# Alternating passes over a K/V cache that keep their last blocks, a running softmax by units, and weight products by head group inside the passes

## The chip, the cores and the metric

One core of a Trainium2 chip runs the whole program. The metric is the device time of one execution in microseconds (us). All runs quoted here are of the state "fast"; every ratio is to runs of the kernel before on the same chip, in the same rounds. Differences in us between two changed kernels are differences of medians, often from other rounds and chips; the median of the kernel before moved by less than 3 us between those (2212 to 2215).

Names: PE is TensorE (matmuls and transposes), DVE is VectorE, ACT is ScalarE, POOL is GpSimd. POOL issues the writes of gradients in program order, SP issues the loads. "Granted clock" is the share of full speed that the throttle gave TensorE.

## The reference

One token goes through attention, a squared-ReLU FFN, attention and FFN again, then backward through all of it. Both attention layers use the same weights and the same K/V cache, and so do both FFN layers.

```python
B, Hq, Hkv, Sk, Dh, D, F = 1, 32, 4, 65536, 128, 1024, 3584      # bf16

def attn(x, k_cache, v_cache, wq, wo):          # 8 query heads for each of 4 groups
    q = (x @ wq).reshape(B, 1, Hq, Dh).transpose(0, 2, 1, 3)
    k, v = jnp.repeat(k_cache, 8, axis=1), jnp.repeat(v_cache, 8, axis=1)
    p = softmax(jnp.einsum("bhqd,bhkd->bhqk", q, k) * Dh ** -0.5)
    return jnp.einsum("bhqk,bhkd->bhqd", p, v).transpose(0, 2, 1, 3).reshape(B, 1, Hq * Dh) @ wo

def ffn(x, w1, b1, w2, b2):
    r = relu(x @ w1 + b1)
    return (r * r) @ w2 + b2

def fwd(x, ...):
    x = x + attn(ln(x));  x = x + ffn(ln(x))
    x = x + attn(ln(x));  return x + ffn(ln(x))

out, vjp = jax.vjp(fwd, ...);  return out, *vjp(grad_out)   # gradients of x, K, V, wq, wo, w1, b1, w2, b2
```

K and V have 67 MB each, and so have their gradients. The rest is small, but it sits between the large passes.

## The kernel before

It reads K and V four times. Pass 1 and pass 2 are the forward attention of the two layers; pass 3 is the backward of the second layer (query gradient only). Pass 4 is the backward of the first layer, and it also computes the K and V gradients of both layers and writes them. Between two passes lies a "dense stretch": weight products, layernorms and row products (a weight row times a vector, summed along the row), a chain in which each step needs the one before.

In pass 4 a step handles 8 chunks of 128 cache rows. Gradients are cast from PSUM into a staging tile `gst` and written when it is full; four tiles of 1 MB take turns:

```python
J = 16                                         # chunks of a K/V block: 512 KB, rows of 4 KB in DRAM
stpool = ctx4.enter_context(tc.tile_pool(name=lname + "_st", bufs=4))
def k8(idx):                                   # [cut: query gradient]
    if j0 == 0:
        state["st"] = stpool.tile([P, 2, J, DH], BF, name="gst", tag="gst")
    for half in range(2):
        pgs = [ps_gg(), ps_gg()]               # four PSUM buffers of 512 columns
        # ... two matmuls with 64 partitions, then one cast for each into gst
    if j0 + 8 == J:
        nc.gpsimd.dma_start(out=GKv[g][b], in_=st[:, 0, :, :])
        nc.gpsimd.dma_start(out=GVv[g][b], in_=st[:, 1, :, :])
```

The weight gradients are sums of two outer products (one for each layer). They run in the background of pass 4, one PSUM tile of 512 columns in each step; the two row vectors lie in rows padded with zeros to 128 partitions:

```python
rows = pool.tile([P, 32 * P], BF, name=name, tag=tag)
nc.gpsimd.memset(rows[:, 0:n], 0.0)            # 126 of 128 partitions are zero
...
nc.tensor.matmul(pg[:, 0:nn], lhsT=st["a"][:, kb * P:(kb + 1) * P], rhs=st["b"][:, n0:n0 + nn], ...)
evac(stg[:, n0:n0 + nn], pg[:, 0:nn])
# ... when the row of tiles is complete:
nc.gpsimd.dma_start(out=out_dram[kb * P:(kb + 1) * P, :], in_=stg[:, 0:N])

def bg(i):                                     # called once a step; per_step is 1 here
    if i < 4: return
    for _ in range(per_step):
        t = next(tasks, None)
        if t is not None: t()
```

## Time and profile before

| kernel | us, median (range) | span | bytes moved | granted clock over pass 4 |
|---|---|---|---|---|
| before | 2212 (2208 to 2216) | 2209.8 | 825.6 MB | 0.96 |

The page's row of GB/s (40 equal slices of 55 us) and of TensorE's clock:

```profile
PEclk9999995579999955599999965899999899999976
GB/s 369 359 409 407 406 394 357 372 340 310 407 407 398 387 328 391 295 382 407 406 404 402 396 295 282 282 414 404 353 415 418 373 401 406 413 402 417 412 294 228
```

The plateau of the passes is 404 to 409 GB/s, in pass 4 up to 418; the dips are the dense stretches (282 to 295), the start of pass 2, where nearly all loads are of K (310), and the tail (228). Stretches cut by hand (columns: from and to, length, busy time and instructions of PE, weight loads, DVE, ACT and POOL, then clock, DMA share, GB/s). Here are the third dense stretch and pass 4:

```profile
1277.00:1400.00 123.00, 74.53 (x889) 61.49 (x890) 95.23 (x191) 79.22 (x97) 4.98 (x4) 0.53 0.72 261
1400.00:2128.00 728.00, 603.32 (x8062) 367.50 (x8059) 555.71 (x969) 455.84 (x817) 268.82 (x500) 0.96 1.01 399
```

### The profile page before, as it was taken

What the parts mean: (1) busy time and instruction counts of PE and PEld (TensorE: products, weight loads), DVE (VectorE), ACT (ScalarE), POOL (GpSimd) and SP (SyncE); (2) the same over time, 40 slices, a digit from 0 to 9 for tenths busy, and PEclk for the clock granted to TensorE, in tenths of its full rate; (3) what the DMA queues carried; (4) which work ended last, traced back from release to release, by engine and by line L of the source; (5) the groups of instructions that cost most, each with busy time, mean ns of one, the idle gap of its engine ahead of it and who ended that gap; (6) DMA issues with size and microseconds to landing.
All of it is one profiled execution on the core that took longest, in us unless ns stands there. A gap on an engine that the chain in (4) does not pass through costs nothing. (4 is left out here: it accounts for less than half of the span.)

```text
span 2209.8 us, 69246 instructions
## 1 busy us (share of the span) xinstructions
PE 1712.9 (78%) x30344; PEld 1338.0 (61%) x30344; DVE 1202.4 (54%) x2148; ACT 1002.5 (45%) x1532; POOL 281.4 (13%) x524
## 2 busy tenths in 40 slices
PE   6888876578888863688888866778888878788875
PEld 5877775568777753577777755444454444455542
DVE  3544430445434300753444367877887777777776
ACT  2543440325434400543333357566566566666654
POOL 0000000000000000000000000243333333343320
PEclk9999995579999955599999965899999899999976
DMA  9999999988999999899999977799999999999976
GB/s 369 359 409 407 406 394 357 372 340 310 407 407 398 387 328 391 295 382 407 406 404 402 396 295 282 282 414 404 353 415 418 373 401 406 413 402 417 412 294 228
DMA packets 229106, 825.57 MB, mean 374 GB/s; under 512 B 23748, under 2 KB 23748, under 8 KB 223684
## 3 DMA queue, kind: packets, MB, share of 16 engines
q1 hardware_dynamic: 184836, 655.46, 76.7%
q0 software_dynamic: 43968, 165.70, 18.6%
q8 instruction: 237, 3.88, 0.7%
q14 instruction: 65, 0.53, 0.1%
HBM read 655.37 MB, written 165.69 MB: 372 GB/s over the span
## 5 line engine op out<-in xcount | busy, mean ns | idle before, releaser
L177 DVE COPY kt<-ps_tr 128x1024 bf16<-128x1024 bf16 x482 | 331.6, 688 | 256.5 <-PE ps_tr L459 135.1
L174 ACT CAST gst<-ps_gg 128x512 bf16<-128x512 f32 x607 | 323.5, 593 | 191.7 <-PE ps_gg L789 144.1
L177 DVE CAST gst<-ps_gg 128x512 bf16<-128x512 f32 x417 | 273.0, 686 | 82.1 <-PE ps_gg L789 51.7
L174 ACT COPY kt<-ps_tr 128x1024 bf16<-128x1024 bf16 x158 | 159.9, 1013 | 312.8 <-PE ps_tr L459 149.0
L177 DVE COPY kt<-ps_gr 128x1024 bf16<-128x1024 bf16 x245 | 168.3, 687 | 172.2 <-PE ps_gr L459 97.3
L459 PEld LDWEIGHTS <-kblk 128*128 128x128 bf16 x4096 | 239.8, 99 | 15.6 <-DMA kblk<-in_A_k_cache_dram 13.9
L478 PE MATMUL ps_sc<-L_qpad,kt 128*128 128x64 bf16 x4096 | 202.9, 195 | 59.3 <-DVE kt L177 49.1
L174 ACT COPY kt<-ps_gr 128x1024 bf16<-128x1024 bf16 x139 | 140.7, 1012 | 212.6 <-PE ps_gr L459 106.5
L789 PE MATMUL ps_gg<-GG,xt 64*128 64x512 bf16 x1024 | 193.6, 394 | 43.9 <-ACT og L174 15.1
L723 PEld LDWEIGHTS <-vblk 128*128 128x128 bf16 x2048 | 137.7, 100 | 141.9 <-issue 127.9
L478 PEld LDWEIGHTS <-kt 128*128 128x128 bf16 x4096 | 160.5, 99 | 84.8 <-DVE kt L177 67.7
L522 PEld LDWEIGHTS <-vblk 128*128 128x128 bf16 x4096 | 172.7, 105 | 54.2 <-DMA vblk<-in_A_v_cache_dram 52.0
L723 PE MATMUL ps_tr<-ident_b,vblk 128*128 128x128 bf16 x2048 | 183.1, 226 | 5.7 <-ACT xt L174 4.8
L352 ACT ACTIVATE junka<-mvt_t 128x1024 bf16<-128x1024 bf16 (+2 forms) x88 | 139.9, 1590 | 101.7 <-DVE mvt_t L351 89.4
L756 POOL COPY X<-eT_123 128x200 bf16<-128x200 bf16 x88 | 46.6, 530 | 984.7 <-ACT junka L352 943.2
L459 PE MATMUL ps_tr<-ident_b,kblk 128*128 128x128 bf16 x2048 | 161.1, 223 | 9.9 <-DMA kblk<-in_A_k_cache_dram 7.8
L459 PE MATMUL ps_gr<-ident_b,kblk 128*128 128x128 bf16 x2048 | 159.8, 221 | 0.0
L624 PEld LDWEIGHTS <-vblk 128*128 128x128 bf16 x2048 | 116.8, 99 | 19.5 <-DMA vblk<-in_A_v_cache_dram 14.3
L522 PE MATMUL ps_acc<-eT_124,vblk 128*128 128x64 bf16 x2048 | 103.2, 209 | 27.5 <-DMA vblk<-in_A_v_cache_dram 26.6
L359 PE MATMUL ps_tr<-ident_b,w_slab 128*128 128x128 bf16 x776 | 95.0, 303 | 32.0 <-DMA w_slab<-in_B_w_dram 15.1
L783 PE MATMUL ps_acc<-X,kblk 128*128 128x64 bf16 x2048 | 118.5, 196 | 0.0
L174 ACT CAST og<-ps_gg 128x512 bf16<-128x512 f32 x139 | 81.0, 586 | 80.7 <-DMA out_dram<-og 44.5
(255 smaller groups left out, 2466.7 us busy)
## 6 DMA issues: line engine op xcount, KB each, us to landing
kblk<-in_A_k_cache_dram SPq DMA_DIRECT2D x512, 512.0 KB, 9.1
vblk<-in_A_v_cache_dram SPq DMA_DIRECT2D x512, 512.0 KB, 9.0
out_dram<-gst POOLq DMA_DIRECT2D x256, 512.0 KB, 10.4
w_slab<-in_A_wq_dram SPq DMA_DIRECT2D x32, 1024.0 KB, 5.6
w_slab<-in_A_wo_dram SPq DMA_DIRECT2D x32, 1024.0 KB, 10.1
w_slab<-in_B_w_dram SPq DMA_DIRECT2D x32, 896.0 KB, 7.7
w_slab<-in_B_w_dram SPq DMA_DIRECT2D x21, 1024.0 KB, 8.7
out_dram<-og POOLq DMA_DIRECT2D x60, 256.0 KB, 8.5
```

Of the source, the lines that this page charges most:

```text
L174: nc.scalar.copy(out=out, in_=in_)
L177: nc.vector.tensor_copy(out=out, in_=in_)
L352: nc.scalar.activation(out=self.junka[:, 0:N], in_=t[:, 0:N], func=ACTF.Copy, accum_out=self.y[:, kc:kc + 1])
L359: nc.tensor.transpose(pt[:, i, :], slab[:, (g0 + i) * P:(g0 + i + 1) * P], ident_b[:, :])
L459: nc.tensor.transpose(pt[:, i, :], kb8[:, i, :], ident_b[:, :])
L478: nc.tensor.matmul(ps_s[:, slot:slot + 8, :].rearrange("p a b -> p (a b)"), lhsT=kt[:, i, :], rhs=qpad[:, g, :, :].rearrange("p a b -> p ( ...
L522: nc.tensor.matmul(ps_o[:, :, :].rearrange("p a b -> p (a b)"), lhsT=vb8[:, i, :], rhs=eT[:, g, :, c:c + 8], start=(c == 0), stop=(c == C ...
L624: nc.tensor.transpose(pt[:, i, :], vb8[:, i, :], ident_b[:, :])
L723: nc.tensor.transpose(pt[:, i, :], vb8[:, i, :], ident_b[:, :])
L756: nc.gpsimd.tensor_copy(out=X[:, 0:un1, R2:3 * R], in_=ea)
L783: nc.tensor.matmul(ps_dq[:, :, :].rearrange("p a b -> p (a b)"), lhsT=kb8[:, i, :], rhs=X[:, sl:sl + 2, :].rearrange("p a b -> p (a b)"), ...
L789: nc.tensor.matmul(pgs[t2][:, :], lhsT=xt[64 * t2:64 * t2 + 64, blk0 + half, :], rhs=GG[64 * t2:64 * t2 + 64, :, :, :].rearrange("p a b c ...
```

## The change

The intent: move fewer bytes, in larger pieces, with fewer stretches in which the DMA queue idles. Core of the diff:

```diff
-    J = 16                                    # K/V blocks of 512 KB
+    J = 32                                    # 1 MB, rows of 8 KB
+    SU = min(128, C)                          # softmax unit: V follows K by 23 steps, not 78
+    NKEEP = 6;  NSTREAM = 6                   # 1 MB slots; only the 6 "keep" slots exist in pass 4
+    def plan_keep(p):                         # last blocks of a pass that the next, reversed, reads first
+        if p == 3: return set()
+        last = TOUCH[p][-(NKEEP + 4):]
+        return set([k for k in TOUCH[p + 1] if k in last][:NKEEP])

-        stpool = ...tile_pool(name=lname + "_st", bufs=4)     # 4 x 16 chunks (1 MB)
+        stpool = ...tile_pool(name="b4_st", bufs=2)           # 2 x 32 chunks (2 MB), same bytes
-                pgs = [ps_gg(), ps_gg()]                      # 4 PSUM buffers of 512 columns
+                pg = ps_gg()                                  # 2 of 1024, one cast for both products

-        rows = pool.tile([P, 32 * P], BF, ...)
-        nc.gpsimd.memset(rows[:, 0:n], 0.0)
+        rows = pool.tile([2, 8 * P], BF, ...)                 # two partitions, no padding
+                    og = pool.tile([P, 8 * P], BF, name="og", tag="og", bufs=3)

+    class Background:                         # wq and wo by head group run as "urgent" work inside passes
+        def step(self, i):
+            if i < 2: return
+            while self.urgent:
+                if next(self.urgent[0][1], "end") == "end":
+                    self.urgent.popleft(); continue
+                return                        # urgent work first: no outer product in this step
+            want = self.total * (i - 2) / self.steps
+            while self.normal and self.done < want:           # catch up with the schedule
+                if next(self.normal[0], "end") == "end": self.normal.popleft()
+                else: self.done += 1

+            add_load(pe=nbk * 0.064)          # in the weight products: the chooser of row products sees PE as loaded
```

A row product can be done on DVE, on DVE and ACT, or by transposes on TensorE; the "chooser" picks the form from a running count of each engine's load. A "turn" is the change from one pass to the next, which reads the cache in the reverse order.

## The prediction

> **What bounds the kernel.** Bytes. The page gives 825.6 MB in a span of 2209.8 us, 374 GB/s. Busy table by stretches:
>
> | stretch | us | GB/s | DMA share |
> |---|---|---|---|
> | pass 1 and start | 370 | 388 | 0.99 |
> | dense 1-2 | 93 | 355 | 0.94 |
> | pass 2 | 362 | 371 | 0.97 |
> | dense 2-3 | 121 | 339 | 0.91 |
> | pass 3 | 331 | 400 | 1.02 |
> | dense 3-4 | 123 | 261 | 0.72 |
> | pass 4 | 728 | 399 | 1.01 |
> | tail | 82 | 228 | 0.63 |
>
> Inside passes the plateau is 405-407 GB/s with PE 83-86% busy: the DMA engines bind. A step of 24 transposes and matmuls takes PE 0.91 us at best (timeline at 950 us), its data 1.29 us. All bytes at 407 GB/s would take 2028 us; some 180 us are lost in dense stretches, V-only ends (323-331 GB/s), K-only beginnings (281-356) and the tail.
>
> **What the change does.**
> 1. Six kept 1 MB blocks at each of three turns: 18.9 MB fewer reads, 46 us at 407 GB/s; total 807 MB.
> 2. Softmax per 128 chunks: V lags K by 23 steps, not 78, so K-only and V-only stretches nearly vanish (about 35 us of lost DMA time). Price: statistics 16 times a pass, not 4. The present ones make PE wait under 2 us each. ACT is under half busy there: off the critical path.
> 3. Three of four head groups of wq and wo, and the output's w2 product, go into the passes. No byte disappears, but each dense stretch shrinks from 31-39 MB to 18.8 MB (46 us of DMA) beside a chain of layernorms, broadcasts and row products, which I estimate from the timeline's pieces (w1 product 6.4 us, 28 row products 22, layernorm 4-5) at 45, 52 and 78 us. A third is loaded at its start; six further blocks can follow, except before pass 4, whose six slots hold kept blocks. Idle DMA: 5, 8 and 40 us.
> 4. The tail keeps one group of four: 82 -> 30 us.
> 5. Rows of 8 KB instead of 4 KB for K, V and their gradients. The Trainium skill ("DMA: Bandwidth & Descriptors", "Why small descriptors are slow") states a fixed cost per packet. The trace agrees: a 1 MB wo slab of 2 KB rows lands every 2.71 us (387 GB/s), a 0.92 MB w1 slab of 7 KB rows every 2.17 us (422). I count +1.5% (estimate) in passes; wq and its gradient fall to 2 KB rows, -5% on 42 MB.
> 6. Pass 4 evacuates 1024 columns at once (512 casts, not 1024): off the critical path.
>
> **Sum** (estimate; K/V at 412 GB/s, 2 KB rows at 380-390): pass 1 370, pass 2 343, pass 3 362, dense 194, pass 4 745 (304 MB), tail 30: about 2040 us, 8% less. Range 1965 to 2120. Faster by over 2%: 0.94; within 2%: 0.04; slower by over 2%: 0.02.
>
> **What would show it.** Bytes near 807 MB; plateau 410 to 425 GB/s in passes; dense stretches of 45 to 80 us, the third worst with DMA share under 0.6; no 50 us stretch of V-only matmuls; tail near 30 us.
>
> **What would make it wrong.** PE is in order: sixteen statistics chains and in-pass weight products could stall it beyond the 0.38 us of slack per step, leaving passes at 380 GB/s. Two 2 MB gradient buffers in pass 4 could make evacuation wait for writes. Kept blocks may idle the queue at a pass's start, giving their gain back. If 8 KB rows reach 423 GB/s everywhere, about 1990.

## More of the kernel before

Pass 4 has the DMA engines busy from end to end. The waits for buffers on their way out are small there (table of waits: engine, line, what it waited for, us in total, times, longest):

```profile
PE ps_gg L837 <- ACT gst L174: 48.9, 126, 3.6
ACT gst L174 <- DMA out_dram<-gst: 40.1, 21, 4.0
ACT og L174 <- DMA out_dram<-og: 33.2, 22, 2.8
DVE gst L177 <- DMA out_dram<-gst: 23.0, 16, 3.8
DVE og L177 <- DMA out_dram<-og: 21.2, 12, 2.5
```

No single wait of these is longer than 4.0 us.

## The result, and the profile after

The changed kernel took 2180 us (median of 4; 2177.5 to 2181.5) beside 2212. The ratio is 0.985, with a 95% interval of 0.984 to 0.987. That is 1.5% faster where 8% was predicted. 806.5 MB were moved, as predicted.

| stretch | before, us | predicted | after, us |
|---|---|---|---|
| passes 1 to 3, with the start | 1063 | 1075 | 1066 |
| three dense stretches | 337 | 194 | 246 (76, 76, 94) |
| pass 4 | 728 | 745 | 838 |
| tail | 82 | 30 | 28 |

Nearly all of the miss is in pass 4 (93 us over the prediction) and in the dense stretches (52 us over). The page:

```profile
PEclk9999998599999966999999667888888878887888
GB/s 383 418 416 416 418 416 402 310 345 415 419 415 417 417 377 264 406 414 418 416 416 419 315 112 359 318 346 369 386 356 357 347 364 364 379 354 349 396 353 249
```

Passes 1 to 3 confirm the large rows: their plateau is 414 to 419 GB/s where it was 404 to 409, some 2.5% more. From slice 25 on, in pass 4, there is no plateau at all: 318 to 396 GB/s, with TensorE's clock at 0.7 to 0.8 in the row of tenths. Pass 4 by the stretch view:

```profile
1312.00:2150.00 838.00, 688.08 (x8015) 421.26 (x8015) 562.51 (x793) 521.86 (x566) 204.59 (x364) 0.84 0.92 358
```

The DMA share fell from 1.01 to 0.92: the queue has less to do than it could. DVE and ACT are busy for 1084 us together against 1012, only 7% more, in a stretch 15% longer. But their waits for staging have grown (the first two lines: 154 us, where it was 63), and the single waits of TensorE for their casts are longer:

```profile
ACT gst L143 <- DMA out_dram<-gst: 89.9, 26, 6.7
DVE gst L146 <- DMA out_dram<-gst: 64.4, 18, 7.0
PE ps_gg L829 <- ACT gst L143: 56.6, 38, 5.5
PE ps_gg L870 <- ACT gst L143: 22.4, 17, 6.0
PE ps_gg L870 <- DVE gst L146: 16.0, 10, 6.3
```

A cast waits for a gradient write and TensorE waits for the PSUM buffer of that cast. In such a wait the trace shows nothing else on TensorE (7.01 us in the timeline under f1_cap), so the transposes and products that would free K/V blocks wait too. The chain of waits that ended last, which the page could follow back for some 27% of the span, has the writes of K/V gradients as its largest part. (In the kernel before the chain breaks off after 3% of the span, so it is no measure there.)

```profile
DMA out_dram<-gst 10%; PE ps_gg L829 2%; PE ps_tr L769 2%; ACT gst L143 2%; PE ps_gg L870 1%; PE ps_sc L787 1%; PE ps_acc L823 1%; PE ps_tr L802 1%; DVE gst L146 1%; PE ps_sc L784 0%; DMA out_dram<-og 0%; POOL out_dram L836 0%; POOL out_dram L874 0%; PE ps_gg L854 0%; ACT kt L143 0%
```

The size of the staging tile offers an explanation, which e1_half and i1_lo_fine test. Pass 4 fills 64 tiles of 2 MB in about 745 us, 11.6 us each (worked out from the prediction's own pass length). The trace gives 10.4 us from issue to landing of a write. With two tiles, a write must land within one fill, 11.6 us, so any delay is a stall; with four tiles of half the size it has three fills of 5.8 us, 17.5 us. SBUF used is the same. (In g1_even below, with four tiles, a write took 13.7 us to land: more than one coarse fill, less than three fine ones.)

### The profile page after: what moved, and what is told of

Its sections match the earlier page's. It is cut to its first block, busy times and chain, and to the rows that moved or that the text cites. A ratio compares the mean times of both kernels' runs of the same rounds, so it can differ in the third digit from the quotient of the medians.

```text
span 2178.0 us, 66787 instructions
## 1 busy us (share of the span) xinstructions
PE 1713.9 (79%) x29802; PEld 1353.1 (62%) x29802; DVE 1238.8 (57%) x2298; ACT 1081.2 (50%) x1672; POOL 219.6 (10%) x416
## 5 line engine op out<-in xcount | busy, mean ns | idle before, releaser
L143 ACT COPY kt<-ps_tr 128x1024 bf16<-128x1024 bf16 x357 | 357.4, 1014 | 494.8 <-PE ps_tr L524 301.0
L143 ACT CAST gst<-ps_gg 128x1024 bf16<-128x1024 f32 x296 | 296.5, 1016 | 210.2 <-PE ps_gg L829 114.0
L146 DVE CAST gst<-ps_gg 128x1024 bf16<-128x1024 f32 x216 | 262.9, 1220 | 160.4 <-PE ps_gg L829 86.9
L541 PE MATMUL ps_sc<-L_qpad,kt 128*128 128x64 bf16 (+7 forms) x4096 | 196.2, 194 | 19.2 <-DVE kt L146 9.4
L769 PE MATMUL ps_tr<-ident_b,blk 128*128 128x128 bf16 x2048 | 206.7, 243 | 0.9 <-DVE ctd_rows L164 0.4
L769 PEld LDWEIGHTS <-blk 128*128 128x128 bf16 x2048 | 141.4, 108 | 79.7 <-issue 78.6
L524 PE MATMUL ps_tr<-ident_b,blks 128*128 128x128 bf16 x2016 | 150.8, 230 | 30.1 <-DMA blks<-in_A_k_cache_dram 26.6
L524 PE MATMUL ps_tr<-ident_b,blk 128*128 128x128 bf16 x2080 | 148.6, 225 | 17.9 <-DMA blk<-in_A_k_cache_dram 17.4
L524 PEld LDWEIGHTS <-blks 128*128 128x128 bf16 x2016 | 126.5, 104 | 34.6 <-DMA blks<-in_A_k_cache_dram 30.5
L524 PEld LDWEIGHTS <-blk 128*128 128x128 bf16 x2080 | 125.1, 101 | 21.9 <-DMA blk<-in_A_k_cache_dram 20.8
L787 PE MATMUL ps_sc<-DOB,kt 128*128 128x64 bf16 (+3 forms) x2048 | 127.5, 203 | 0.0
L823 PE MATMUL ps_acc<-X,blk 128*128 128x64 bf16 (+1 forms) x2048 | 118.4, 202 | 0.0
L823 PEld LDWEIGHTS <-blk 128*128 128x128 bf16 x2048 | 87.9, 104 | 34.4 <-issue 33.8
## 6 DMA issues: line engine op xcount, KB each, us to landing
out_dram<-gst POOLq DMA_DIRECT2D x128, 1024.0 KB, 10.4
blks<-in_B_w_dram SPq DMA_DIRECT2D x32, 896.0 KB, 10.4
```

Of the source, the lines that this page charges most:

```text
L143: nc.scalar.copy(out=out, in_=in_)
L146: nc.vector.tensor_copy(out=out, in_=in_)
L524: nc.tensor.transpose(pt[:, i, :], kb8[:, i, :], ident_b[:, :])
L541: nc.tensor.matmul(state["ps_s"][:, s:s + w, :].rearrange("p a b -> p (a b)"), lhsT=kt[:, i, :], rhs=L["qpad"][:, g, 0:w, :].rearrange("p ...
L769: nc.tensor.transpose(pt[:, i, :], vb8[:, i, :], ident_b[:, :])
L787: nc.tensor.matmul(state["ps_dp"][:, s:s + w, :].rearrange("p a b -> p (a b)"), lhsT=vt[:, i, :], rhs=DOB[:, g, 0:w, :].rearrange("p a b - ...
```

## The experiments

Eighteen kernels were run. Three theories were named for pass 4 in turn: A, the coarse staging; B, bursts of background tiles; G, TensorE's clock. C (PSUM) and D (row size of the writes) are rivals. E, F and J concern the dense stretches and the kept blocks. In the expectations of e1_half and e2_rows4k, B still stands for another rival, six read slots being too few in pass 4; g1_even later fills the DMA queue with the same six slots, so that one is out.

### e1_half: four staging tiles of 16 chunks, same memory

```diff
-        stpool = ... bufs=2
+        stpool = ... bufs=4
-            if j0 == 0:
-                state["st"] = stpool.tile([P, 2, J, DH], ...)
+            if j0 % 16 == 0:
+                state["st"] = stpool.tile([P, 2, 16, DH], ...)
-            if j0 + 8 == J:                   # write 32 chunks
+            if j0 % 16 == 8:                  # write 16 chunks, rows of 4 KB
```

> Same 32 KB of gradient staging in pass 4, cut into four buffers of 16 chunks (2 x 0.5 MB) instead of two of 32 chunks (2 x 1 MB); writes go out twice as often, with 4 KB rows. Theory A (two coarse staging buffers make the casts wait for the writes, 151 us of such waits in the trace of the changed kernel): pass 4 falls from 838 us to 745-775, the whole from 2178 to 2090-2115, waits of the casts for the writes fall below 60 us. Theory B (six read slots are too few in pass 4): no change, within 10 us. Theory C (PE in order behind two PSUM double banks and the background products): no change. Theory D (8 KB-row writes are slow in themselves): faster too, but then the next run is faster as well.

Measured: 2154 us (2146 to 2156), ratio 0.973 [0.970, 0.975]. A gain of 26 us, a third of what A expected. The waits for `gst` writes fell from 154 to 25 us, but those for the tiles of weight gradients (`og`) grew from 23 to 113 us, and now one of them lasts 17 us:

```profile
ACT og L143 <- DMA out_dram<-og: 69.3, 11, 16.8
DVE og L146 <- DMA out_dram<-og: 43.7, 10, 11.2
ACT gst L143 <- DMA out_dram<-gst: 14.0, 7, 3.5
DVE gst L146 <- DMA out_dram<-gst: 11.0, 4, 4.3
```

A is a cause, and not the only one.

### e2_rows4k: the coarse staging, written with rows of 4 KB

```diff
-                nc.gpsimd.dma_start(out=GKv[g][b], in_=stg[:, 0, :, :])
+                for h0 in (0, 16):            # same moment, two writes
+                    nc.gpsimd.dma_start(out=GKv[g][b][:, h0:h0 + 16, :], in_=stg[:, 0, h0:h0 + 16, :])
```

> Two coarse staging buffers as in the changed kernel, but each is written by four transfers with 4 KB rows at the same moment. Theory A: no gain (2170-2190). Theory D (row size of the writes): as fast as the run with four buffers. Theories B and C: no change.

Measured: 2174 us (2161 to 2180), ratio 0.982 [0.978, 0.986], which overlaps the changed kernel's interval. The size of the rows written is not what e1_half gained by.

### e3_nopeload and e4_nokeep: the dense stretches

```diff
-            add_load(pe=nbk * 0.064)          # e3_nopeload
-        if p == 3: return set()               # e4_nokeep: no block is kept, 825 MB again
+        if p >= 0: return set()
```

> The w1/w2 products no longer count as PE load when the form of a row product is chosen, so the forms by transposes come back. Theory E (in the dense stretches 1-2 and 2-3 the chooser put nearly all row products on DVE at 1.22 us each, which delays the layernorm chain): stretch 1-2 from 76 to 58-65 us, stretch 2-3 from 76 to 62-70, whole 2145-2165. Rival: those stretches are bound by their weight loads; then within 5 us of 2178.

Measured: 2175 us (2174 to 2185), ratio 0.985 [0.981, 0.988]: a miss for E, no gain clear of noise. It is the number that the rival (bound by weight loads) had named, but the queue was not full there, as follows.

> No block is kept at the turns; bytes go back to 825 MB. If the bytes bind everywhere, 46 us slower (2225). Theory F (at each turn the DMA queue is idle anyway, so the kept bytes are worth little): 2170-2195; most of the 18.9 MB are loaded in the idle time of the dense stretches, whose rate rises.

Measured: 2181 us (2180 to 2191), ratio 0.987 [0.984, 0.989], the same as with kept blocks, though 18.9 MB more are read. The same 20 us of the first dense stretch, in the changed kernel and then in e4_nokeep, show why:

```profile
400.00:420.00 20.00, 5.07 (x160) 4.66 (x160) 19.55 (x33) 1.79 (x3) 0.00 (x0) 0.50 0.84 302
```

```profile
400.00:420.00 20.00, 5.06 (x160) 4.66 (x160) 19.55 (x33) 1.71 (x3) 0.00 (x0) 0.50 1.04 393
```

DVE is busy for 19.55 of 20 us in both: the chooser, told that PE is loaded, put the row products there. The chain is equally slow, but without kept blocks the queue has free slots and loads the next pass meanwhile, at 393 instead of 302 GB/s. Over the same three dense stretches (366 to 442, 792 to 868 and 1218 to 1312 us) e4_nokeep moved 395, 379 and 246 GB/s where the changed kernel moved 333, 293 and 183: 17 of the 18.9 MB. A kept block saves its load only if the queue had something else to do. In e3_nopeload the first dense stretch moves more (366 to 442 us at 360 GB/s), but the queue still idles right after the turn, as it does in the changed kernel. First the changed kernel, then e3_nopeload:

```profile
450.00:460.00 10.00, 7.09 (x157) 6.75 (x157) 4.85 (x12) 6.05 (x19) 0.00 (x0) 0.96 0.67 261
460.00:470.00 10.00, 9.88 (x232) 9.69 (x230) 4.13 (x8) 3.53 (x4) 0.00 (x0) 0.87 0.53 193
```

```profile
450.00:460.00 10.00, 10.00 (x249) 9.85 (x248) 5.43 (x8) 7.10 (x21) 0.00 (x0) 0.94 0.36 119
```

The first six blocks are there, and the loads behind them wait for a slot: SP's longest wait between 440 and 470 us is 15.4 us in the changed kernel, 11.8 in e3_nopeload, and 4.2 in e4_nokeep, whose queue moves 415 and 419 GB/s from 450 to 470 us.

### f1_cap and f2_cap_only: at most one background tile a step

In e1_half four stretches of pass 4 had lost the queue (241, 302, 288 and 305 GB/s; the second line, 387, is the recovery after the first):

```profile
1400.00:1440.00 40.00, 34.34 (x328) 20.16 (x329) 22.08 (x31) 21.21 (x23) 12.71 (x23) 0.66 0.71 241
1440.00:1480.00 40.00, 35.32 (x362) 20.14 (x361) 29.62 (x37) 25.15 (x27) 15.69 (x29) 0.83 1.01 387
1560.00:1600.00 40.00, 33.50 (x426) 21.90 (x425) 26.61 (x36) 23.25 (x24) 12.60 (x23) 0.87 0.84 302
1760.00:1800.00 40.00, 27.82 (x321) 17.04 (x319) 20.31 (x27) 19.96 (x21) 9.69 (x18) 0.76 0.78 288
1960.00:2000.00 40.00, 30.49 (x311) 17.85 (x310) 23.24 (x32) 19.89 (x21) 11.88 (x22) 0.71 0.82 305
```

They come after stretches of urgent row products, and the code of `Background.step` says why: while urgent work is there, no outer product is given out, but the debt grows by 0.52 tiles a step. Thirty steps of wo row products make 15 tiles, all due in one step. The changed kernel's own trace shows it: between 1382 and 1432 us no K/V gradient is written, and 15 tiles of 256 KB go out through three buffers. Its timeline (start, duration, what, and in brackets the idle time before it and what ended that):

```profile
1397.09 0.60 PE L870 MATMUL ps_gg<-rowb,rowa 2*128 2x512 bf16 x2
1405.22 1.23 DVE L146 CAST og<-ps_gg 128x1024 bf16<-128x1024 f32 x1 [6.52 <-DMA out_dram<-og]
1406.50 2.07 PE L870 MATMUL ps_gg<-rowb,rowa 2*128 2x512 bf16 x4 [7.01 <-DVE og L146]
1406.51 1.01 ACT L143 CAST og<-ps_gg 128x1024 bf16<-128x1024 f32 x1 [9.47 <-DVE og L146]
```

```diff
-            while self.normal and self.done < want:
+            if self.normal and self.done < want:
```

> On top of e1_half, the background schedule gives out at most one outer-product tile per step. Theory B (bursts): the schedule counts its debt by steps, but gives out nothing while a row product of wq or wo is in its urgent queue; after the 30 steps of the three wo row products it then emits 15 tiles at once into three staging buffers, and 5 or 6 after each group of wq. In e1_half four stretches of 40 us (from 1400, 1560, 1760 and 1960 us) moved only 241, 302, 288 and 305 GB/s; against 400 that is 16 + 10 + 11 + 10 = 47 us. B expects 2154 -> 2110 us (2095 to 2130) and no stretch under 350 GB/s in the middle of pass 4. Theory G (TensorE's clock, lowered by outer products from two partitions) and theory C (two wide PSUM buffers instead of four narrow ones) expect 2145 to 2155.

Measured (on top of e1_half): 2139 us (2135 to 2142), ratio 0.967 [0.966, 0.969]. 15 us better, where B expected 44. The stretches shrank but stayed: paying the debt with one tile in every step is still too much.

> The same one-tile-per-step limit alone, on the changed kernel with its two coarse staging buffers. Theory B: 2180 -> 2145 us (2130 to 2160), and with e1_half's 26 us the two gains roughly add. If the coarse buffers were the cause of most of the loss by themselves: 2170 to 2180.

Measured (alone on the changed kernel): 2175 us (2154 to 2184, a wide range), ratio 0.980 [0.975, 0.985]. A miss: alone it gives little, its interval touches the changed kernel's. While the coarse staging is there, it hides most of what the limit gains.

### f4_cap_pad and f5_cap_gg512: the clock, and PSUM

```diff
-        rows = pool.tile([2, 8 * P], BF, name=tag, tag=tag)        # f4_cap_pad, on f1_cap
+        rows = pool.tile([P, 8 * P], BF, name=tag, tag=tag)
+        nc.gpsimd.memset(rows[:, :], 0.0)
-        ps_gg: 2 buffers of [P, 1024]                              # f5_cap_gg512, on f1_cap
+        ps_gg: 4 buffers of [P, 512], a cast for each
```

> f1_cap with the rows of the outer products padded with zeros to 128 partitions, as in the kernel before. Theory G: the granted clock in pass 4 returns from 0.84 to about 0.95 and the time falls 15 us or more below f1_cap. Theory B: the clock was low because TensorE stood still and came back at half speed, so f1_cap alone raises it; f4_cap_pad within 6 us of f1_cap.

Measured: 2119 us (2114 to 2120), ratio 0.958 [0.956, 0.959]. 20 us better than f1_cap, as G expected. I cut pass 4 into windows of 1 us and counted those with a granted clock below 0.75 ("half clock"), and the falls (a window below 0.75 after one that is not); the last but one column is their quotient:

| kernel | us at half clock | falls | us for each fall | mean clock |
|---|---|---|---|---|
| before | 64 of 728 | 11 | 5.8 | 0.96 |
| after | 271 of 820 | 31 | 8.7 | 0.83 |
| e1_half | 250 of 790 | 26 | 9.6 | 0.84 |
| f1_cap | 219 of 780 | 23 | 9.5 | 0.86 |
| f4_cap_pad | 127 of 760 | 20 | 6.4 | 0.92 |

The falls are about as many with and without padding (23 and 20), but with two-partition rows each half-clock stretch is longer. The trace of f1_cap after a stall of 7 us shows half speed for 11 us of nearly unbroken work: a pair of outer products takes 1.02 us, a later one 0.59.

```profile
1598.67 0.61 PE L829 MATMUL ps_gg<-GG,xt 64*128 64x512 bf16 x2 [6.95 <-ACT og L143]
1602.36 1.02 PE L870 MATMUL ps_gg<-rowb,rowa 2*128 2x512 bf16 x2
1610.98 0.59 PE L870 MATMUL ps_gg<-rowb,rowa 2*128 2x512 bf16 x2
```

> f1_cap with four PSUM buffers of 512 columns and one eviction for each, as in the kernel before, instead of two of 1024. Theory C: matmuls of the next half can start while a cast runs, TensorE's waits for gst and og casts shrink, and the time falls 15 us or more below f1_cap. Theory B alone: within 8 us of f1_cap, or slower, as 512 more casts with their fixed cost load ACT and DVE.

Measured: 2135 us (2127 to 2141), ratio 0.965 [0.963, 0.968], the same as f1_cap. C is out.

### g0_pad and h1_b2row: the padding alone, and its mirror

> Only the zero padding of the outer products' rows to 128 partitions, on the changed kernel as it is (coarse staging, bursts). Theory G (two-partition matmuls do not keep TensorE's clock up): f4_cap_pad against f1_cap was 0.9576 to 0.967, 21 us; the clock in pass 4 was half for 271 of 820 us in the changed kernel, 30 drops of 9 us. Alone it should give 10 to 20 us: 2180 -> 2160 to 2170, clock in pass 4 from 0.83 to 0.88. If the padding only worked together with the other two edits: 2175 to 2182.

Measured: 2174 us (2171 to 2181), ratio 0.982 [0.980, 0.985]. Alone the padding gives about 6 us, below the 10 to 20 that G expected, and the interval overlaps the changed kernel's (0.984 to 0.987), so even that is not clear of noise. The clock in pass 4 is 0.86, and TensorE is busy there for 653 us instead of 688: 35 us less of busy TensorE bought about 6 us.

```diff
-        rows = pool.tile([P, 32 * P], BF, name=name, tag=tag)      # h1_b2row: kernel before
-        nc.gpsimd.memset(rows[:, 0:n], 0.0)
+        rows = pool.tile([2, 32 * P], BF, name=name, tag=tag)
```

> The mirror on the kernel before: its outer products' rows cut to two partitions, nothing else. Theory G: the granted clock in pass 4 falls from 0.96 to 0.90 or less, drops last 9 to 10 us instead of 6, and pass 4 gets slower by 8 to 20 us: 2212 -> 2218 to 2232. If the two-partition rows are harmless and f4_cap_pad won by something else, such as the zero fills on POOL: 2208 to 2216, the clock unchanged.

Measured: 2225 us (2210 to 2231), ratio 1.004 [1.000, 1.008]. Half clock rose from 64 to 141 us with 13 falls (10.8 us each), mean clock 0.90. So two-partition rows do keep the clock down, in either kernel. Here the low clock has a price of its own: one of the 13 half-clock stretches lasts 41 us, with TensorE busy for nearly all of it, and the queue falls to 255 GB/s (one stretch, in the one run that was profiled):

```profile
1584.00:1624.00 40.00, 39.35 (x283) 20.27 (x282) 24.31 (x48) 17.91 (x32) 9.35 (x19) 0.50 0.69 255
```

Against 400 GB/s that is some 15 us (estimate from this line).

### g1_even: no debt

```diff
             while self.urgent:
                 if next(self.urgent[0][1], "end") == "end":
                     self.urgent.popleft(); continue
-                return
+                break                         # a tile may follow in the same step
```

> f4_cap_pad with the background queue giving a row-product step and an outer-product tile in the same step, so no debt builds up. f4_cap_pad still paid the debt of 15 tiles with 30 steps of one tile each: 256 KB more per step, 1400 to 1520 us at 362 to 386 GB/s, and 1560 to 1600 at 328. Theory B: these stretches rise to 400 and the time falls by 8 to 15 us to 2104 to 2111. If the number of og buffers is the limit even without debt: within 5 us of 2119.

Measured (with finer staging, one-tile limit and padding): 2100 us (2098 to 2102), ratio 0.949 [0.947, 0.950]. Better than B's range. At the places where e1_half had lost the queue it is now full (391 to 401 GB/s in all four; two of them here):

```profile
1400.00:1440.00 40.00, 35.22 (x475) 22.81 (x477) 31.11 (x41) 30.39 (x33) 16.14 (x29) 1.00 1.02 398
1760.00:1800.00 40.00, 33.62 (x431) 21.77 (x433) 28.62 (x36) 26.14 (x27) 14.45 (x27) 0.96 1.02 396
```

### i1_lo_fine, i2_lo_pad, i3_lo_even: each cause put back alone

The gains so far depended on the order of the edits. So each was taken out of g1_even by itself.

> g1_even with the changed kernel's two coarse staging buffers put back: padding and even background stay. If coarse staging is a cause by itself, the casts wait for gradient writes again (150 us of waits in the changed kernel) and the time rises by 20 to 35 us over g1_even's 2100. If the burst was what made the writes late: within 8 us of 2100.

Measured: 2135 us (2130 to 2141), ratio 0.966 [0.963, 0.968]: 35 us lost. The casts wait for gradient writes again:

```profile
ACT gst L143 <- DMA out_dram<-gst: 96.1, 33, 6.6
DVE gst L146 <- DMA out_dram<-gst: 87.6, 29, 6.0
```

In g1_even these two waits were short:

```profile
ACT gst L143 <- DMA out_dram<-gst: 38.0, 19, 3.6
DVE gst L146 <- DMA out_dram<-gst: 20.2, 12, 2.7
```

> g1_even without the padding: fine staging and even background stay. If two-partition outer products cost by themselves, the clock in pass 4 falls from 0.935 to about 0.86 and the time rises by 12 to 25 us over 2100. If they only made the way back from a long stall slower, and the stalls are gone: within 8 us of 2100.

Measured: 2100 us (2098 to 2103), ratio 0.950 [0.948, 0.952]: nothing lost. The clock is lower (0.90 against 0.935; 24 falls of 6.1 us instead of 18 of 5.3), and it does not matter here, as the DMA queue is full in both. Pass 4 in g1_even, then in i2_lo_pad:

```profile
1318.00:2073.00 755.00, 616.92 (x7966) 401.02 (x8054) 569.89 (x795) 520.91 (x562) 293.44 (x514) 0.93 1.01 399
```

```profile
1318.00:2070.00 752.00, 647.93 (x8020) 400.87 (x8019) 565.12 (x788) 518.95 (x556) 268.58 (x487) 0.90 1.01 399
```

> g1_even with the held-back background and its bursts put back: fine staging and padding stay. If the bursts cost by themselves: 25 to 40 us over 2100 (the four stretches of e1_half lost 47 us together, of which the padding saves some by a faster return to full clock). If they cost only at a half clock: within 10 us.

Measured: 2138 us (2135 to 2140), ratio 0.967 [0.965, 0.969]: 38 us lost. The long waits for `og` writes are back:

```profile
ACT og L143 <- DMA out_dram<-og: 74.3, 11, 16.2
DVE og L146 <- DMA out_dram<-og: 43.3, 9, 13.6
```

| taken out of g1_even (2100 us) | us | loss |
|---|---|---|
| finer staging (i1) | 2135 | 35 |
| even background (i3) | 2138 | 38 |
| padding (i2) | 2100 | 0 |

Coarse staging and bursts are causes; in this kernel the low clock is a companion. With stalls there, the padding was worth up to 20 us (f4_cap_pad against f1_cap); in g1_even, with the stalls gone, it is worth nothing. That overturns G as a cause of its own here, which f4_cap_pad's 20 us had seemed to show. It is no general rule: in h1_b2row the same two-partition rows cost some 9 us by the ratio, just clear of noise, in a kernel with neither coarse staging nor bursts.

### i4_g1_nk, g2_even_rp, g3_even_rp_nk, i5_best: kept blocks and the chooser again

> g1_even, with the row products of the dense stretches allowed their transposing forms again and no kept blocks. Each alone gave nothing (e3 2175, e4 2181 beside 2180). Theory J: they are one trade. A shorter chain has no data to load while the slots hold kept blocks, and free slots have no time to gain while the chain is long; together the dense stretches lose their idle DMA, 30 to 50 us by the slices (1240 to 1320 us ran at 135 to 176 GB/s), less 19 MB read again (45 us): within 12 us of g1_even. If keeping is worth its bytes: 20 us or more slower than g1_even.

Measured: 2093.5 us (2092.6 to 2096.0), ratio 0.946 [0.945, 0.947].

> g1_even without kept blocks, the chooser as changed. Theory J (kept blocks and a slow chain are one trade: whatever is not read again is idle time in the dense stretch): within 6 us of 2100, and g3_even_rp_nk's 6 us are the chooser's. If dropping the kept blocks alone gives the gain: 2092 to 2095.

Measured: 2093 us (2091 to 2097), ratio 0.947 [0.945, 0.949]. No kept blocks and the chooser as changed: all of g3's gain. J had put that gain down to the chooser; that part of J is wrong.

> g1_even with the transposing row products allowed again, six blocks kept. Theory J: a shorter chain finds nothing to load, as every slot holds a kept block or a weight still in use, so its gain comes back as an idle queue at the turn: within 5 us of 2100. If the chain's length is what costs in the dense stretches: 2080 to 2090.

Measured: 2097 us (2096.6 to 2099.4), ratio 0.948 [0.946, 0.950]. The shorter chain gives 3 us by the medians while blocks are kept (the intervals overlap, so this is not shown), and nothing without them. The core of J holds: keeping six blocks was worth nothing, and perhaps 4 to 7 us less than nothing (the intervals of i4 and g1_even overlap a little).

> g3_even_rp_nk with four buffers for weight-gradient tiles instead of three. In g1_even ACT and DVE still waited 50 us for tile writes, but the queue was full at 400 GB/s in nearly all of pass 4. If DMA bandwidth is what is left there: 2090 to 2095, the same as g3. If the tile buffers still hold the casts back: 2078 to 2088.

Measured: 2088 us (2087.3 to 2088.4), ratio 0.944 [0.942, 0.946]. A fourth `og` buffer gives some 5 us beside g3 by the medians, which come from different rounds; their intervals overlap, so this last step is likely, not shown. The version that the runs point to is 5.6% faster than the kernel before and 4.2% faster than the change as made (by the medians, 2088 over 2180). Its third dense stretch still idles: from 1260 to 1320 us it moves 108, 107 and 254 GB/s in thirds, which against 400 is 37 us. Whether that chain can be shortened was not tried.

## Why the prediction was wrong

- **Bytes and plateau: right.** 806.5 MB, and 414 to 419 GB/s in passes 1 to 3, against 404 to 409 before. The named range was 410 to 425. Their sum was 1066 us, predicted 1075.
- **The tail: right.** 28 us, predicted 30.
- **"PE is in order: sixteen statistics chains ... could stall it": did not happen.** The passes with statistics ran at the plateau.
- **The step that failed: "pass 4 745 (304 MB)".** That term divided bytes by a bandwidth, as if nothing between the casts and the writes could fall behind. Pass 4 took 838 us. Two causes are shown. The two 2 MB staging tiles cost 35 us with all else mended (i1); finer ones gained 26 us as the first thing mended (e1). The prediction named this risk, "Two 2 MB gradient buffers in pass 4 could make evacuation wait for writes", but gave it no time. It could have been sized: 10.4 us to land (the same in the kernel before) against one fill of 11.6 us.
- **The bursts were missed altogether.** They cost 38 us (i3). They stand in the diff: a queue that is not served while its debt grows, and a `while` that pays it in one step. The prediction looked at what the background work adds, not when it comes.
- **"Pass 4 evacuates 1024 columns at once ... off the critical path": half wrong.** The width was harmless: going back to 512 columns changed nothing (f5). But the casts did hold TensorE up, as they waited for staging (TensorE's waits for `gst` casts in the lines above: 95 us), so evacuation was not off the critical path. In the kernel before such waits were shorter: 49 us in 126 waits, none above 3.6 us, for the largest group.
- **Two partitions instead of 128 in the outer products: overlooked.** In kernels with long stalls it lengthened the mean half-clock stretch from 6 or 7 us to 9 or 10. As long as there were stalls this cost from 6 us, not clear of noise (g0), to 20 us (f4 against f1), and 0 in g1_even without them (i2).
- **"Six kept 1 MB blocks at each of three turns: ... 46 us at 407 GB/s": wrong.** The worth was 0 (e4) or a few us below 0 (i4). The bytes are saved, but in stretches where a serial chain, not the queue, sets the time; without them, the free slots load ahead at 393 GB/s. The prediction listed this as a risk and counted the full gain all the same.
- **"dense 194": 246.** The chains were priced from a mix of row products over PE, DVE and ACT. The one line that adds PE load in the weight products made the chooser put them on DVE (19.55 of 20 us busy). Allowing the mix again gained nothing clear of noise (e3, g2: 3 to 4 us by the medians), and dropping the kept blocks 4 to 7 us at most (i4). The prediction's own terms (46 us of loads in each stretch, and 5, 8 and 40 us of idle queue) put most of the miss into the first two stretches: 76, 76 and 94 us were measured. So a longer chain than the 45 and 52 us that I had summed there is the likely rest; it was not tested, and this part stays open.

Together g1_even's edits gave 80 us (in its trace pass 4 takes 755 us, where 745 had been predicted and 838 measured), and i5_best at 2088 us lies within the predicted range. The goal of the change was within reach; the arrangement of buffers and background work missed it.

## What to carry to other kernels

Before a buffer is made larger and fewer at equal memory, compare the time to fill one with the time for its write to land: N buffers give a write N - 1 fills (of such arrangements only two large tiles and four small ones were tried). Background work that may be held back must not be paid back at once, and had better run beside the urgent work. Price saved bytes only where the queue is what binds, and take each cause out of the mended kernel singly: a gain measured on a broken one may belong to a companion.

## What the Trainium skill lacked or had wrong

- "TensorE: Matmul & The Clock Gate", section "Part 1: The HAM clock gate", says that the clock halves after an idle window of about 3.4 us and returns after at least one busy window of that length. The traces agree on the two speeds and on the length: cut into windows of 0.25 us, the half-clock stretches of pass 4 last 3.25 to 3.5 us, 6.75 to 7, 10 to 10.25 and so on, multiples of 3.4 (nine kernels: before, after, e1, f1, f4, g0, g1, h1 and i2). But a window need not be idle throughout: before its falls TensorE had idled for 1.1 to 2.9 us of the last 4 us in the kernel before, and in the changed kernel four falls followed 0.4 to 0.7 us (as the trace models busy time). And one busy window is often not enough where outer products have two partitions: in h1_b2row a half-clock stretch lasted 40.75 us with TensorE busy for 40.1. The page does not say that the number of filled partitions matters; h1_b2row shows it (64 to 141 us at half clock by that edit alone).
- The same page, "Part 3: Packing small matmuls", says that with fewer than 128 partitions most of the array sits idle. It could add that such products also seem to count for little towards full clock (again h1_b2row: mean clock of pass 4 0.90, where it was 0.96).
- "DMA: Bandwidth & Descriptors", section "Where 436 GB/s comes from", says that for transfers between HBM and SBUF the HBM side, about 358 GB/s, binds. This core alone held a plateau of 414 to 419 GB/s in passes 1 to 3. "Perfetto Trace Analysis", section "Roofline", which puts a single core's practical ceiling near 120% of 358, is the one that fits (419 is 117%).
- "DMA: Bandwidth & Descriptors", section "Why small descriptors are slow", agrees with the loads (8 KB rows some 2.5% faster than 4 KB), though other things changed with them, so no run here shows how much of it the rows gave. For writes of gradients 4 KB and 8 KB rows made no difference that the runs could tell (e2: 2174 against 2180).
- No page gives a rule for the number of staging buffers against the latency of a write: 10.4 us to land for 1 MB writes, in a queue full of reads.
